# Sparse attention and feed-forward on one core: the scores of two head units joined in one TensorE segment, their loads cut by unit, and the agenda set anew

## The chip, the core and the metric

The kernel runs on one core of a Trainium2 chip. The engines of a core work side by side: TensorE (PE in the profile, its weight loads PEld) multiplies, VectorE (DVE), ScalarE (ACT) and GpSimd (POOL) do elementwise work, SyncE (SP) issues most transfers. The metric is the device time in microseconds, lower is better; the kernel before takes 816.55 us, the median of three runs.

## The reference

```python
# q, k, v: 8 batches, 8 heads, 576 positions, 64 wide; w_in 512 x 2048, w_out 2048 x 512
scores = q @ k.T / 8
local   = (0 <= i - j) & (i - j < 32)              # heads 0 to 3
strided = (0 <= i - j) & (i % 32 == j % 32)        # heads 4 to 7
attn = softmax(where(mask, scores, -1e9)) @ v
x = attn, heads side by side: 4608 tokens x 512
h = x @ w_in
g = where(h >= 1, h, where(h <= -1, 0, (h + 1)**2 / 4))
out = g @ w_out
```

All of it is float32. The kernel splits each factor of the feed-forward's products into a rounded part and a remainder and adds three products, so one product of 128 x 128 by 128 x 512 is three matmuls.

## The kernel before

**Feed-forward.** TensorE's time is mostly the feed-forward. The first three chunks of 512 tokens go the plain way (functions `up`, `gate`, `rounded`, `down`, matmuls on lines 775 and 820), one step for each of the 16 blocks of 128 hidden columns. The other 3072 tokens go in three blocks of 1024 (`up_block`, line 917; `down_block`, line 1005) by a scheme with seven products in place of eight. Its factors are read back from DRAM through a ring of seven buffers of 256 KB (tiles `wr`): each product, when done, lets SP fetch the factor that is used seven products later (`fetch_w`, line 845). The factors `kq` and `ks` are written to DRAM in the first phase (`ship`, `ship_sums`, on ACT's queue; a `ks` ship is 1 MB).

**Attention.** Batch by batch, while the feed-forward of earlier tokens runs. The heads go two and two (pairs p = 0, 1, each on two halves j = 0, 1 of the partitions), and the queries of the local and of the strided heads are cut into two units each. Counted from zero these are the units 0 and 1 (local: 12 and 6 blocks of 32 queries by 64 keys) and 2 and 3 (strided: 6 and 5 blocks of 54 keys). In the words of the change, units two and four are numbers 1 and 3. A step is a letter with a unit's number:

- `s` scores (TensorE, line 482), into two PSUM banks, one for each j
- `m` adds the mask out of PSUM into `pr` (DVE, line 542), which frees the two banks
- `x` row maximum, `a` or `b` subtracts it (POOL or DVE), `e` the exponential (ACT), `q` the sum, `p` or `k` adds the epsilon (ACT or DVE), `r` or `w` divides (POOL or DVE)
- `t` transposes blocks of 32 (DVE), `j` writes them to DRAM (SP, line 643, `there<-t`), `J` gathers them as `pT` (SP, line 654, `pT<-there`, four DMAs)
- `v` the product with the values (TensorE, line 669); `V` does units 1 and 3 in one go
- `h`, `l` copy the result out of PSUM (ACT; DVE for the remainder where one is kept)
- `Q0`, `Q2` load q and k (SP, line 418), `F0` to `F4` the values (line 431)

Batches 0 and 1 use a shorter way on TensorE for the transposes (`f`, line 609) and do v1 and v3 apart.

**Banks and buffers.** The scores and value products of all batches from 1 on share two PSUM banks, a0 and a1, taken in turn: a segment on TensorE starts only when the readers of the segment before it are done. The tile pool for q and k (`qk_p`) has two buffers. Before, each holds one pair of heads over all columns: `Q0` loads the two pairs of local heads (576 KB each) for units 0 and 1, `Q2` the two of strided heads (604 KB each) for units 2 and 3.

**Order.** All of it is written out by hand. `BEGIN` is the order of the opening; `WORK` gives each attention step of batches 1 to 7 a time, `SUMS`, `SHIP` and `CONV` those of the weights' preparation, `X_WORK` and `G_WORK` those of the splits and sums in the blocks of 1024. These times count groups of six large matmuls, from zero where the second chunk begins; 128 is the start of the blocks. `until(t)` issues every step with a time below t between two groups. The list fixes the order on every engine and in SP's queue. A step can run earlier than its time on an engine that has nothing to wait for; TensorE's steps stand where they are put, and in the blocks SP is held to TensorE's pace by the ring.

Of the kernel before, what the change touches and what calls it, by code (L numbers as in the profile page):

```python
# [28 lines left out]
BEGIN = """
Zs0:17 o0 s0 o1 i0 X0 s1 i1 S0 o3 g1 x1 s2 Zv0:3 Zf0:3 m2 e0 a1 A00 s3 i3 e1 x2 q0 p0 g3 a2 q1 Zf0:9  # L30
e2 w0 Zf0:5 f0 p1 x3 c0 B00 v0 b3 L00 e3 r1 q2 p2 f1 C00 r2 q3 A10 d1 D00 p3 h0 r3 L10 l0 A20 v1 B10
f2 h1 d2 f3 c3 v3 l1 H1 L20 C10 G10 v2 E10 M0 M1 h3 B20 l3 E00 h2 H3 C20 U0 l2 G20 V0 M3 U1 H2 M2
E20 V1
"""
# [62 lines left out]

# [1078 lines left out]
```

## Time and profile before

| what | value |
|---|---|
| median of 3 runs | 816.55 us (816.5 to 817.0) |
| profiled execution | 817.29 us |
| its span, first to last instruction | 815.5 us |
| TensorE busy | 806.2 us, 6969 matmuls |
| DVE, ACT, POOL busy | 574.7, 495.4, 232.5 us |
| moved by DMA | 195.10 MB |

The profiled execution's time is its span and 1.8 us around it. In the lines below, a group has its source line, engine, operation, output and inputs, shapes and count; in the timeline a row has its start, its length from the first start to the last end, and the instructions merged into it. Neighbouring matmuls overlap, so the next row starts before the one above it has ended, and the cost of a segment is read from start to start. A row such as `64*32 64x64` is a matmul with 64 rows and 32 columns of weights and 64 columns of data; each float32 product of the attention is two such instructions. The chain of waits lists, back from the last instruction of a window, what released each step.

### The profile page before, as it was taken

The page shows a single profiled execution, that of the slowest core. Times are in us where ns is not written, and L with a number is a line of the kernel's source. Part 1 is how long each engine was busy: PE and PEld are TensorE (multiplying, and loading weights), DVE is VectorE, ACT ScalarE, POOL GpSimd, SP SyncE. Part 2 cuts the span into 40 slices and gives each one's busy share as a digit, 9 for nine tenths or more (in the row PEclk, how much of TensorE's full clock was granted, in tenths as well). Part 3 has the DMA queues.
Part 4 walks back from the last instruction along what each step waited for, and adds up shares of the span by engine and source line. Part 5 has one row for each costly group of instructions (what it writes and reads, how often), then busy time and mean ns, then how long its engine had stood idle before and what let it go on. Part 6 is the DMA issues. An engine that isn't in the chain of part 4 may idle for free.

```text
span 815.5 us, 17861 instructions
## 1 busy us (share of the span) xinstructions
PE 806.2 (99%) x6969; PEld 656.9 (81%) x6969; DVE 574.7 (70%) x850; ACT 495.4 (61%) x866; POOL 232.5 (29%) x226
## 2 busy tenths in 40 slices
PE   8999999999999999999999999999999999999998
PEld 6788888878878888887878888888888888888886
DVE  5898868767548477776778876675589834558664
ACT  5888955545355365776775453778654647775442
POOL 5353544873347543023222000220120001114100
PEclk9999999999999999999999999999999999999999
DMA  9936437788868867987998768887666776666765
GB/s 344 408 138 201 153 111 274 265 298 278 265 221 299 286 243 257 304 287 247 285 288 266 216 203 249 263 265 228 193 193 213 232 235 196 196 192 190 216 200 170
DMA packets 101796, 195.10 MB, mean 239 GB/s; under 512 B 17105, under 2 KB 32465, under 8 KB 99665
## 3 DMA queue, kind: packets, MB, share of 16 engines
q1 hardware_dynamic: 92496, 164.60, 63.3%
q10 hardware_dynamic: 9216, 29.36, 9.4%
q8 instruction: 55, 0.90, 0.5%
q14 instruction: 29, 0.23, 0.1%
HBM read 147.26 MB, written 46.66 MB: 238 GB/s over the span
## 4 chain that ended last, share of the span: by engine, by line
PE 91%; DMA 5%; issue 1%; DVE 1%; ACT 1%; POOL 0%; SPq 0%; ACTq 0%; POOLq 0%
PE o L820 16%; PE h L775 16%; PE yo L1005 15%; PE y L917 15%; PE zo L1005 8%; PE z L917 7%; PE xo L1005 4%; PE x L917 4%; PE xp L669 3%; PE sc L482 3%; DMA wr<-kq 1%; DMA qk<-in_qk_s 1%; DMA there<-t 1%; DMA pT<-there 1%; DMA qk<-in_qk_l 1%
## 5 line engine op out<-in xcount | busy, mean ns | idle before, releaser
L917 PE MATMUL y<-x,wr 128*128 128x512 f32 x576 | 141.3, 392 | 0.0
L775 PE MATMUL h<-xq,w 128*128 128x512 f32 x576 | 140.0, 392 | 0.1
L1005 PE MATMUL yo<-hl,wr 128*128 128x512 f32 x576 | 132.8, 390 | 0.6 <-DMA wr<-kq 0.6
L820 PE MATMUL o<-gh,w 128*128 128x512 f32 x384 | 130.1, 399 | 0.0
L1005 PEld LDWEIGHTS yo<-hl,wr 128*128 128x128 f32 x576 | 108.0, 188 | 23.4 <-DMA wr<-kq 1.0
L775 PEld LDWEIGHTS h<-xq,w 128*128 128x128 f32 x576 | 107.4, 188 | 23.4 <-DVE xq L739 0.7
L917 PEld LDWEIGHTS y<-x,wr 128*128 128x128 f32 x576 | 107.4, 188 | 22.7
L820 PEld LDWEIGHTS o<-gh,w 128*128 128x128 f32 x384 | 72.1, 188 | 16.2
L820 PE MATMUL o<-gl,w 128*128 128x512 f32 x192 | 75.0, 391 | 0.0
L917 PE MATMUL z<-x,wr 128*128 128x512 f32 x288 | 73.7, 391 | 0.0
L957 POOL TENSOR_TENSOR ga<-gb,ga 128x1024 f32<-128x1024 f32 x9 | 21.6, 2397 | 167.5 <-DVE ga L785 141.7
L1005 PE MATMUL zo<-hl,wr 128*128 128x512 f32 x288 | 66.1, 390 | 0.0
L572 POOL TENSOR_TENSOR pr<-pr,st 128x384 f32<-128x384 f32 (+3 forms) x21 | 26.3, 1253 | 135.7 <-DVE st L595 64.5
L1005 PEld LDWEIGHTS zo<-hl,wr 128*128 128x128 f32 x288 | 54.0, 188 | 11.3
L917 PEld LDWEIGHTS z<-x,wr 128*128 128x128 f32 x288 | 53.8, 188 | 11.3
L782 ACT ACTIVATE tmp<-tmp 128x512 f32<-128x512 f32 x96 | 60.7, 632 | 3.0
L871 DVE TENSOR_TENSOR hl<-ga,hl 128x1024 fp32r<-128x1024 f32 x36 | 47.3, 1315 | 19.9 <-ACT hl L870 18.2
L870 ACT CAST hl<-ga 128x1024 fp32r<-128x1024 f32 x36 | 38.0, 1056 | 35.1 <-PE yo L1005 12.6
L396 POOL TENSOR_TENSOR xs<-w 128x512 f32<-128x512 f32 x32 | 45.1, 1426 | 48.4 <-DMA ks<-xs 32.8
L785 DVE SCALAR_TENSOR_TENSOR h<-h,u 128x512 f32<-128x512 f32 x47 | 32.8, 697 | 30.5 <-ACT u L782 30.1
L398 POOL TENSOR_TENSOR xs<-xs 128x256 f32<-128x256 f32 x64 | 51.3, 802 | 5.0
L779 ACT ACTIVATE u<-h,half 128x512 f32<-128x512 f32 x48 | 33.1, 689 | 29.6 <-PE h L775 24.1
(120 smaller groups left out, 1321.9 us busy)
## 6 DMA issues: line engine op xcount, KB each, us to landing
wr<-ks SPq DMA_DIRECT2D x192, 256.0 KB, 3.9
wr<-kq SPq DMA_DIRECT2D x144, 256.0 KB, 3.4
...
qk<-in_qk_s SPq DMA_DIRECT2D x16, 604.0 KB, 6.1
...
v<-in_v_l SPq DMA_DIRECT2D x21, 384.0 KB, 6.0
```

The lines of the kernel that those rows point to most:

```text
L396: nc.gpsimd.tensor_tensor(out=b[:, :, f] if i else b[:, f], in0=hi, in1=lo, op=ALU.add)
L398: nc.gpsimd.tensor_tensor(out=st[:, to, HF:], in0=st[:, x, HF:], in1=st[:, y, HF:], op=op)
L572: eng.tensor_tensor(out=pr, in0=pr, in1=st[:, 0].unsqueeze(2).broadcast_to(list(pr.shape)), op=ALU.add)
L775: nc.tensor.matmul(o_ps[c, f], wt[f][:, 0, h, x, e:e + P], xq[c][:, y, cc], start=first and n == 0, stop=last and n == len(todo) - 1)
L779: nc.scalar.activation(u, h, AF.Relu, bias=half, scale=0.5)
L782: nc.scalar.activation(u, u, AF.Square)
L785: nc.vector.scalar_tensor_tensor(out=to, in0=h, scalar=1.0, in1=u, op0=ALU.max, op1=ALU.min)
L820: nc.tensor.matmul(o_ps[c][d], wt[f][:, 1, h, x, e:e + P], gs[y], start=f == 0 and n == 0, stop=f == NF - 1 and n == 2)
L870: nc.scalar.copy(t[:, 0], src)
L871: nc.vector.tensor_tensor(out=t[:, 1], in0=src, in1=t[:, 0].bitcast(F32), op=ALU.subtract)
L917: nc.tensor.matmul(to, w_[:, a, c * P:(c + 1) * P], xc[m][:, b, c], start=m in (1, 2, 5) and c + q == 0, stop=c == 1 and q == 2, skip_grou ...
L1005: nc.tensor.matmul(to, w_[jj][:, a, d * P:(d + 1) * P], t[:, b, jj], start=m in (1, 2, 5) and k + jj + q == 0, stop=k == NP // 2 - 1 and j ...
```

## The change

From batch 2 on, the step `s3` issues the scores of unit 1 and then those of unit 3. Both lie in the same two banks: unit 1's full slot in columns 0 to 127, its half slot from column 128, unit 3's full slots from column 256, and its half slot in the same columns as unit 1's, on the other partitions. For that, unit 3's half slot swaps the halves of the partitions between j = 0 and 1 (`half_of`). The step `s1` is gone from batches 2 to 7; `m1` and `m3` stay two steps.

q and k are laid out by unit on the host: `qk_0` for unit 0 (384 columns), `qk_2` for unit 2 (334), `qk_13` for units 1 and 3 side by side (224 + 280). From batch 2 on there are three loads a batch, each for two pairs of heads: `Q0`, `Q2` and `Q3`, of 2 x 384, 2 x 342 and 2 x 516 KB. Batches 0 and 1 load as before.

The order of a batch from 2 on is then s0, s2, v0, s3 (with s1), v2, V, where it was s0, s1, s2, v0, s3, v2, V. The times in `WORK` from batch 2 on are new; so are `SUMS`, `SHIP`, `X_WORK`, `G_WORK`, a few in `CONV`, the two constants `GATE` and `ROUNDED`, and the end of `BEGIN` on DVE and ACT.

```diff
-GATE, ROUNDED = (0.31, 2.01), (1.62, 3.18)
+GATE, ROUNDED = (0.31, 1.87), (1.62, 3.26)
...
- 2: [(-13.48, 'F0'), (-11.61, 'Q0'), (-6.26, 'F1'), (0.1, 's0'), (0.19, 'm0'), ... (2.76, 's1'), ... (5.69, 'Q2'),
-     ... (10.93, 's2'), ... (17.04, 'v0'), ... (19.7, 'l0'), (20.13, 's3'), ... (37.36, 'v2'), ... (44.62, 'V1'), ...
+ 2: [(-11.46, 'Q0'), (-9.5, 'F0'), (-6.26, 'F1'), (0.1, 's0'), (0.11, 'Q2'), (0.19, 'm0'), ... (4.16, 's2'), (4.69, 'Q3'),
+     ... (16.05, 'v0'), ... (18.64, 'l0'), ... (20.17, 's3'), (21.8, 'm1'), ... (39.02, 'v2'), ... (50.62, 'V1'), ...
- 3: [(26.83, 'Q0'), (29.08, 's0'), (37.27, 'm0'), ... (40.48, 's1'), ... (43.81, 'Q2'), ... (48.59, 's2'), ...
-     (57.71, 's3 m3'), ... (59.19, 'v0'), ... (71.29, 'v2'), ...
+ 3: [(24.63, 'Q0'), (27.77, 's0'), (31.29, 'Q2'), (37.63, 'm0'), ... (40.49, 's2'), ... (43.06, 'Q3'), ...
+     (57.32, 's3'), (57.61, 'm1'), ... (57.78, 'm3'), ... (59.09, 'v0'), ... (71.0, 'v2'), ...
- 4: [(57.8, 'Q0'), (72.56, 's0'), ... (77.35, 's1'), ... (80.1, 'Q2'), ... (84.42, 's2'), ... (95.51, 's3'), ... (117.48, 'V1'), ...
+ 4: [(57.93, 'Q0'), (72.56, 's0'), ... (72.74, 'Q2'), ... (77.27, 's2'), ... (80.58, 'Q3'), ... (95.37, 's3'), ... (119.3, 'V1'), ...
- 5: [... (113.91, 's0'), ... (128.62, 'J0'), ... (135.2, 'v0'), ... (154.56, 'j3'), ... (156.06, 'J3'), ...
+ 5: [... (111.18, 's0'), ... (128.62, 'J0'), ... (134.35, 'v0'), ... (156.25, 'j3'), ... (157.1, 'J3'), ...
- 6: [... (152.17, 's0 m0 x0'), ... (158.36, 'Q2'), ... (163.66, 's2'), ... (190.07, 'j3'), ... (193.3, 'J3'), ... (198.39, 'V1'), ...
+ 6: [... (151.1, 's0'), ... (151.15, 'Q2'), ... (156.05, 's2'), (156.3, 'Q3'), ... (193.66, 'j3'), ... (194.58, 'J3'), ... (198.53, 'V1'), ...
- 7: [(183.43, 'Q0'), ... (264.44, 'J2'), ... (270.63, 'v2'), ...
+ 7: [(186.43, 'Q0'), ... (257.42, 'J2'), ... (269.93, 'v2'), ...
...
+    def half_of(u, j):
+        return 1 - j if u == 3 else j
     def seat(u, n, j):
         I = IL if UNITS[u][0] else IS
         s, i = divmod(n, I)
-        return (j, s, i) if s < UNITS[u][2] // I else (0, s, i + j * I // 2)
+        return (j, s, i) if s < UNITS[u][2] // I else (0, s, i + half_of(u, j) * I // 2)
...
+    QK = {0: qk_0, 2: qk_2, 3: qk_13}
+    COLS_1 = S - UNITS[1][1] * QL + ST
+    def load_qk(b, g, p):
+        src = QK[g][b, p]
+        t = qk_p.tile([P, 2, src.shape[2]], F32, tag="qk", name=f"qk_{b}_{g}_{p}")
+        nc.sync.dma_start(t, src)
+        for u, x in ((g, t),) if g < 3 else ((1, t[:, :, :COLS_1]), (3, t[:, :, COLS_1:])):
+            loaded[b, u, p, "qk"] = x
...
+        def score(u):
+            us = (1, 3) if b > 1 and u == 3 else (u,)
+            if len(us) > 1:
+                ts = [psum("a", [P, CH], f"sc_{b}_{u}_{j}") for j in range(2)]
+                def view(t, at, n, W):
+                    return t[:, at:at + n * 2 * W].rearrange("p (n h w) -> p n h w", h=2, w=W)
+                ahead[1, "s"] = [(view(t, 0, 1, WL), view(t, 2 * WL, 1, WL)) for t in ts]
+                ahead[3, "s"] = [(view(t, 4 * WL, 2, WS), view(t, 2 * WL, 1, WS)) for t in ts]
+            for u in us:
+                score_of(u)
...
+    U1, U3 = 12 * QL, 6 * WS
+    qk_0, qk_2 = qk_l[..., :U1], qk_s[..., :U3 + 64 - WS]
+    qk_13 = np.concatenate([qk_l[..., U1 - ST:], qk_s[..., U3:]], 4)
```

More of the change, by code (lines that the diff above doesn't have):

```diff
@@ L22 @@
 CLASSIC = 3
-GATE, ROUNDED = (0.31, 2.01), (1.62, 3.18)
+GATE, ROUNDED = (0.31, 1.87), (1.62, 3.26)
 BEGIN = """
[L30 to L33, printed above, removed]
-"""
-WORK = {1: [(-60.38, 's0'), (-55.74, 'm0'), (-55.4, 'x0'), (-52.6, 'a0'), (-51.93, 's1'), (-51.84, 'Q2'), (-51.74, 'e0 q0'),
[60 rows of a table removed]
-SUMS = [((0, 0), 30.03, 34.27, 34.91, 37.39), ((1, 1), 64.0, 67.03, 67.68, 74.53), ((0, 0), 16.76, 22.19, 23.74, 27.21),
[5 rows of a table removed]
-X_WORK = {0: [(104.12, 1), (105.35, 2), (120.26, -7), (123.3, 7), (123.54, -6), (124.89, -5), (127.46, 6), (127.6, 5),
-     (129.94, 3), (131.5, -4), (134.1, 4)],
- 1: [(196.58, 1), (203.12, 2), (203.92, -7), (211.17, 7), (211.24, -6), (216.29, -5), (218.76, -4), (220.88, 5),
-     (225.52, 6), (231.99, 3), (237.02, 4)],
- 2: [(314.25, 1), (315.57, -7), (318.67, 7), (320.48, -6), (327.96, 2), (328.63, -4), (329.29, -5), (334.12, 5),
-     (337.09, 3), (339.07, 6), (347.97, 4)]}
+Zs0:17 o0 s0 o1 i0 X0 s1 i1 S0 o3 g1 x1 s2 Zv0:3 Zf0:3 m2 e0 s3 a1 A00 i3 e1 x2 q0 p0 g3 a2 q1 Zf0:9
+e2 w0 Zf0:5 f0 p1 x3 c0 B00 v0 b3 L00 e3 r1 q2 p2 f1 C00 r2 q3 A10 d1 D00 p3 h0 r3 L10 l0 v1 B10 f2
+A20 h1 d2 f3 c3 v3 l1 H1 L20 C10 G10 v2 E10 M0 M1 h3 l3 B20 h2 E00 H3 C20 U0 l2 G20 H2 V0 M3 U1 V1
+M2 E20
+"""
+WORK = {1: [(-60.38, 's0'), (-55.74, 'm0'), (-55.4, 'x0'), (-52.6, 'a0'), (-51.93, 's1'), (-51.84, 'Q2'), (-51.74, 'e0'),
[62 rows of a table added]
+SUMS = [((0, 0), 27.43, 34.14, 34.48, 36.04), ((0, 1), 41.64, 42.75, 44.37, 45.37), ((0, 0), 20.89, 22.91, 23.78, 26.47),
[5 rows of a table added]
+X_WORK = {0: [(99.95, 2), (105.24, 1), (120.26, -7), (123.38, -6), (123.76, 7), (124.89, -5), (127.46, 6), (127.62, 5),
+     (128.98, -4), (130.46, 3), (133.39, 4)],
+ 1: [(188.28, 1), (202.28, -7), (203.39, 2), (210.65, 7), (211.24, -6), (212.76, -5), (217.38, -4), (220.5, 5),
+     (224.44, 6), (225.88, 3), (237.31, 4)],
+ 2: [(314.63, 1), (318.5, -7), (320.68, 7), (320.87, -6), (327.96, 2), (328.59, -5), (328.74, -4), (334.45, 5),
+     (337.29, 3), (338.84, 6), (349.14, 4)]}
 CONV = [(-63.99, 'L0.1'), (-63.97, 'A0.1 B0.1'), (-63.52, 'A1.1'), (-63.03, 'C0.1'), (-62.58, 'A3.0'), (-62.43, 'D0.1'),
@@ L132 @@
  (-23.81, 'B12.0'), (-23.64, 'L11.1'), (-23.56, 'B11.1'), (-23.42, 'L13.0'), (-23.33, 'C12.0'), (-23.26, 'C11.1'),
[2 rows of a table removed]
[2 rows of a table added]
  (-18.75, 'D13.0'), (-18.25, 'C12.1'), (-17.87, 'A14.0'), (-17.83, 'D12.1'), (-16.23, 'E13.0'), (-16.16, 'L14.0'),
[4 rows of a table removed]
[4 rows of a table added]
  (-8.08, 'C15.1'), (-7.92, 'D15.1'), (-7.81, 'E15.1')]
-G_WORK = {0: [(165.99, 's11'), (167.56, 's10'), (183.93, 's12'), (187.61, 's20'), (187.74, 's13'), (188.3, 't60'),
[26 rows of a table removed]
-SHIP = [[1.27, 12.82, 7.42, 20.53, 13.61, 18.54, 30.97, 29.74, 34.32, 31.23, 40.56, 58.58, 43.6, 47.29, 57.58, 63.72],
- [67.18, 66.59, 57.74, 75.26, 81.54, 83.67, 98.23, 100.97, 96.76, 104.83, 107.05, 116.41, 110.54, 116.4, 120.59,
+G_WORK = {0: [(166.13, 's11'), (171.17, 's10'), (184.17, 's12'), (185.93, 's13'), (186.58, 's20'), (186.8, 't60'),
[26 rows of a table added]
+SHIP = [[1.76, 9.43, 4.16, 9.04, 7.71, 16.78, 30.13, 28.39, 27.95, 31.89, 43.05, 58.54, 41.31, 47.29, 57.58, 59.69],
+ [65.08, 59.34, 57.19, 75.01, 81.48, 84.8, 98.23, 98.51, 98.16, 100.44, 109.9, 118.16, 110.44, 117.42, 120.59,
   125.26]]
@@ L178, in tile_sparse_attention_then_ffn @@
     qk_s: bass.AP,
+    qk_0: bass.AP,
+    qk_2: bass.AP,
+    qk_13: bass.AP,
     v_l: bass.AP,
@@ L189, in tile_sparse_attention_then_ffn @@
     nc = tc.nc
-    B, _, _, _, S = qk_l.shape
+    B = qk_0.shape[0]
     DM, NT = out.shape
+    S = NT // B
     NF = w.shape[0]
@@ L410, in tile_sparse_attention_then_ffn, with load_pair @@
     loaded = {}
-    def load_qk(b, p):
+    QK = {0: qk_0, 2: qk_2, 3: qk_13}
+    COLS_1 = S - UNITS[1][1] * QL + ST
+    def load_pair(b, p):
         src = qk_l[b, p] if p < 2 else qk_s[b, p - 2]
@@ L418, in load_qk @@
         nc.sync.dma_start(t, src)
-        loaded[b, p, "qk"] = t
+        first = (0, S - COLS_1) if p < 2 else (0, UNITS[3][1] * WS)
+        for u, c in zip((0, 1) if p < 2 else (2, 3), first):
+            loaded[b, u, p % 2, "qk"] = t[:, :, c:]
+    def load_qk(b, g, p):
[4 more added lines that the diff above has]
+            loaded[b, u, p, "qk"] = x
     def load_v(b, u, k=None):
@@ L433, in load_v, with fetch_qk @@
             loaded[b, local, b0 + n] = t[:, n]
-    def fetch_qk(b, p0):
-        for p in (p0, p0 + 1):
-            if b < B and (b, p, "qk") not in loaded:
-                load_qk(b, p)
+    def fetch_qk(b, g):
+        for p in range(2):
+            if b < B and (b, g, p, "qk") not in loaded:
+                (load_pair(b, g + p) if b < 2 else load_qk(b, g, p))
     def fetch_v(b, *parts):
@@ L446, in attention @@
     def attention(b, kinds):
-        probs, flipped, there, ahead, covered = {}, {}, {}, {}, set()
+        probs, flipped, there, ahead, whole, covered = {}, {}, {}, {}, {}, set()
         def banks(u, kind):
@@ L467, in zero @@
                 nc.tensor.matmul(t[:, :N], zeros, zeros[:, :1].broadcast_to([P, N]), start=True, stop=True)
-        def score(u, pairs=range(2)):
-            local, b0, nb = UNITS[u]
-            Q, W, I, p0 = (QL, WL, IL, 0) if local else (QS, WS, IS, 2)
-            if 0 in pairs:
-                probs[u] = banks(u, "s"), W
-            sc = probs[u][0]
-            for p in pairs:
-                for n in range(nb):
-                    q0 = (b0 + n) * (QL if local else WS)
-                    k0 = max(q0 - ST, 0) if local else q0
-                    for j in range(2):
-                        _, s, i = seat(u, n, j)
-                        qk = loaded[b, p0 + p, "qk"][j * D:(j + 1) * D]
-                        nc.tensor.matmul(sc[j][i * Q:(i + 1) * Q, s, p], qk[:, 0, q0:q0 + Q],
-                                         qk[:, 1, k0:k0 + W], start=u not in covered,
-                                         stop=u not in covered)
@@ L486, in score_0 @@
-        def score_0(u):
-            score(u, (0,))
-        def score_1(u):
-            score(u, (1,))
+        def score(u):
[8 more added lines that the diff above has]
+                score_of(u)
@@ new lines, in score_of @@
+        def score_of(u):
+            local, b0, nb = UNITS[u]
+            Q, W, I = (QL, WL, IL) if local else (QS, WS, IS)
+            sc = banks(u, "s")
+            if not isinstance(sc[0], tuple):
+                n = slots(u)[1]
+                whole[u] = sc
+                sc = [(t[:, :n], t[:, n:] if n < t.shape[1] else None) for t in sc]
+            probs[u] = sc, W
+            first_col = (max(b0 * QL - ST, 0) if local else b0 * WS)
+            todo = [(p, n, j) for p in range(2) for n in range(nb) for j in range(2)]
+            for p, n, j in todo:
+                q0 = (b0 + n) * (QL if local else WS)
+                k0 = max(q0 - ST, 0) if local else q0
+                q0, k0 = q0 - first_col, k0 - first_col
+                _, s, i = seat(u, n, j)
+                last = s >= slots(u)[1]
+                qk = loaded[b, u, p, "qk"][j * D:(j + 1) * D]
+                nc.tensor.matmul(sc[j][last][i * Q:(i + 1) * Q, s - last * slots(u)[1], p], qk[:, 0, q0:q0 + Q],
+                                 qk[:, 1, k0:k0 + W], start=u not in covered,
+                                 stop=u not in covered)
@@ L501, in cover @@
             local, b0, _ = UNITS[u]
-            sc, W = probs[u]
+            W = probs[u][1]
             n = slots(u)[0]
             m = m_loc[:, b0 and 1:][:, :n].unsqueeze(2) if local else m_str.unsqueeze(1).unsqueeze(1)
-            for t in sc:
+            for t in whole[u]:
                 nc.tensor.matmul(t, ident_b, m.broadcast_to([P, n, 2, W]), start=False, stop=True)
@@ L524, in homes @@
             if ns[0] > ns[1]:
-                todo += [(j, slice(j * 64, j * 64 + 64), ns[1], ns[0], ns[1]) for j in range(2)]
+                todo += [(j, slice(h * 64, h * 64 + 64), ns[1], ns[0], ns[1]) for j, h in ((j, half_of(u, j)) for j in range(2))]
             pieces_ = []
@@ L528, in homes @@
                 of = part, slice(2 * at, 2 * (at + s1 - s0))
-                pieces_.append((sc[j][part, s0:s1], pr[of].rearrange("p (n h) w -> p n h w", h=2), part, of[1]))
+                pieces_.append((sc[j][s0 >= ns[1]][part, s0 - ns[1] * (s0 >= ns[1]):s1 - ns[1] * (s0 >= ns[1])], pr[of].rearrange("p (n h) w -> p n h w", h=2), part, of[1]))
             return room, st, pr, pieces_
@@ L745, in in_two @@
             return lambda u: do(u, rest if b == 0 else None)
-        steps = {"s": score, "y": score_0, "z": score_1, "m": mask, "o": opened, "i": cover, "g": plain, "X": most_there, "S": below_there, "x": most, "w": norm_v, "a": below_max, "e": expo, "q": total, "p": plus_eps, "k": plus_eps_v, "b": below_max_v, "r": norm,
+        steps = {"s": score, "m": mask, "o": opened, "i": cover, "g": plain, "X": most_there, "S": below_there, "x": most, "w": norm_v, "a": below_max, "e": expo, "q": total, "p": plus_eps, "k": plus_eps_v, "b": below_max_v, "r": norm,
                  "f": flip, "t": turn, "j": spread, "J": gather, "c": keep, "d": keep_v, "v": value, "V": values_1_3, "h": in_two(high, False), "l": in_two(low, False), "H": in_two(high, True), "M": in_two(low, True),
@@ L1043, in tile_sparse_attention_then_ffn @@
     with tc.manual_schedule():
-        for p in range(4):
-            load_qk(0, p)
-        load_w(0, 0, loaded[0, 1, "qk"][0:1, 0, 0:1])
+        for g in (0, 2):
+            fetch_qk(0, g)
+        load_w(0, 0, loaded[0, 0, 1, "qk"][0:1, 0, 0:1])
         load_v(0, 0)
@@ L1053, in tile_sparse_attention_then_ffn @@
         stage(4)
-        for p in range(2):
-            load_qk(1, p)
+        fetch_qk(1, 0)
         stage(6)
@@ L1154, in _layout @@
     w = np.concatenate([w_in, w_out.reshape(DFF // P, P, DM)], 2)
-    return {"qk_l": qk_l, "qk_s": qk_s, "v_l": v_l, "v_s": v_s, "w": w}
+    return {"qk_l": qk_l[:2], "qk_s": qk_s[:2], "qk_0": qk_0, "qk_2": qk_2, "qk_13": qk_13, "v_l": v_l, "v_s": v_s, "w": w}
 def kernel(**inputs):
```

198 rows, old and new, of tables (CONV, G_WORK, SUMS, WORK) are left out of this document.

## The prediction

> **What bounds the kernel.** I read the page first, then the waits of TensorE, then its timeline around the attention's short matmuls, then the chain of waits in the few places where such a segment is longer than its like.
>
> ```profile
> span 815.5 us, 17861 instructions
> PE 806.2 (99%) x6969; PEld 656.9 (81%) x6969; DVE 574.7 (70%) x850; ACT 495.4 (61%) x866; POOL 232.5 (29%) x226
> ```
>
> TensorE is busy 806.2 of 815.5 us: the idle 9.3 us, the opening and the end included, are all that a wait shown as idle could give back. DVE, ACT and POOL have room. So the time changes by what TensorE's own stream costs, and by waits that hide inside "busy", where a segment of short matmuls is stretched. No matmul is removed: the 116 score products a batch stay. What can shrink is the cost of going from 512-column matmuls to short ones and back, and waits inside segments. Next, TensorE's timeline in batch 7, where units two (x48 of 64*32) and four (x40 of 64*64) are scored apart:
>
> ```profile
> 503.05 1.52 PE L917 MATMUL z<-x,wr 128*128 128x512 f32 x6
> 504.50 0.77 PE L482 MATMUL sc<-qk 64*32 64x64 f32 x48
> 505.20 3.03 PE L917 MATMUL y<-x,wr 128*128 128x512 f32 x12
> 508.06 1.52 PE L917 MATMUL x<-x,wr 128*128 128x512 f32 x6
> 509.43 1.52 PE L917 MATMUL z<-x,wr 128*128 128x512 f32 x6
> ...
> 530.03 0.92 PE L482 MATMUL sc<-qk 64*64 64x54 f32 x40
> 530.88 1.66 PE L917 MATMUL x<-x,wr 128*128 128x512 f32 x6
> 532.37 1.52 PE L917 MATMUL z<-x,wr 128*128 128x512 f32 x6
> ```
>
> Undisturbed, six large matmuls take 1.36 us from start to start (508.06 to 509.43); that is one unit of the agenda, and below a "unit" is always this. Six before a segment take 1.45 (503.05 to 504.50), so entering costs 0.09. Twelve after one take 2.86 instead of 2.72 (505.20 to 508.06), six take 1.49 (530.88 to 532.37), so leaving costs 0.13. That is 0.22 us a segment beside the short matmuls.
>
> **The merged segment.** From batch 2 on, unit four's scores follow unit two's in one segment: six segments fewer in all. The trace has the same join for the values, where step V takes units two and four together, while batch 1 takes them apart:
>
> ```profile
> 83.97 0.90 PE L669 MATMUL xp<-pT,v 64*64 64x32 f32 x48
> 84.80 0.50 PE L820 MATMUL o<-gh,w 128*128 128x512 f32 x1
> ...
> 106.44 0.81 PE L669 MATMUL xp<-pT,v 54*64 54x64 f32 x40
> 107.19 2.11 PE L775 MATMUL h<-xq,w 128*128 128x512 f32 x8
> ...
> 562.56 1.51 PE L669 MATMUL xp<-pT,v 64*64 64x32 f32 x88
> 564.00 1.66 PE L917 MATMUL z<-x,wr 128*128 128x512 f32 x6
> ```
>
> Apart, the short matmuls hold TensorE 0.83 and 0.75 us (to the next large one's start), together 1.44: 0.14 less, and with the 0.22 of one entry and exit 0.36 a batch. This is the nearest row, but there all weights are 64 columns wide; the merged scores go from 64*32 to 64*64, which no row shows. If that step costs a whole drain, only the 0.22 is left. Between 0.22 and 0.36 I take 0.30, nearer to the join that the trace shows: 6 x 0.30 = 1.8 us less (1.3 to 2.2).
>
> The Trainium skill, TensorEngine Tiling (Array Packing), Key Properties, states that a change of the tiling mode drains TensorE. By that rule the step inside the merged segment drains once more, and this term would be 1.3 us; the join of the values, which has no such change, doesn't contradict it.
>
> The flip of the half slot in unit four moves which rows write which half of the bank; the tiles are used as often as before, so I put it at nothing. Masks for both units now follow one segment:
>
> ```profile
> 187.12 0.99 DVE L542 TENSOR_TENSOR pr<-sc,m_loc 128x128 f32<-128x128 f32 x4
> 211.16 1.15 DVE L542 TENSOR_TENSOR pr<-sc,m_str 128x216 f32<-128x216 f32 x4 [2.21 <-PE sc L482]
> ```
>
> 0.99 + 1.15 = 2.14 us of DVE before both banks are free. The tightest user is batch 3's v0, two units (2.72) after s3: hidden, 0.6 left. What is queued behind them on DVE, the gate of the step, feeds matmuls eight units later. The swaps between engines (a/b, p/k, r/w) are hidden likewise.
>
> **Waits that the new agenda takes away.** Four segments of before are longer than their like:
>
> ```profile
> 176.20 1.52 PE L775 MATMUL h<-xq,w 128*128 128x512 f32 x6
> 177.81 1.38 PE L669 MATMUL xp<-pT,v 54*64 54x64 f32 x48
> ...
> 546.06 1.39 PE L669 MATMUL xp<-pT,v 54*64 54x64 f32 x48
> 96.60 0.93 PE L669 MATMUL xp<-pT,v 54*64 54x64 f32 x48
> 386.10 1.25 PE L482 MATMUL sc<-qk 64*64 64x54 f32 x48
> 513.60 0.92 PE L482 MATMUL sc<-qk 64*64 64x54 f32 x48
> 153.30 1.08 PE L482 MATMUL sc<-qk 64*64 64x54 f32 x40
> 177.24 0.94 DVE pr L542 x2
> 379.97 6.77 DMA qk<-in_qk_s
> ```
>
> Batch 2's v2 (177.81) is 0.45 longer and starts 0.16 late (1.61 after 176.20): the chain puts batch 3's m0 on DVE before it, which held the banks. v2 goes from 37.36 to 39.02 with m0 at 37.63, so m0 is over: 0.61 back. Batch 7's v2 (546.06) is 0.46 longer; the chain has the gather J2 before it, which goes from 264.44 to 257.42 while v2 stays within a unit: back. Batch 6's s2 (386.10) waited 0.33 for q and k, issued behind gathers; Q2 now stands right behind s0 at 151.15, five units ahead of s2: back. Batch 2's s3 (153.30) is 0.16 longer, by the order of DVE behind l0, which frees its banks; l0 now moves ahead of a chunk step's rounding (19.7 to 18.64): back. Sum 1.56; the bound from below is 0.
>
> The one wait for ring weights lies behind batch 7's first q and k:
>
> ```profile
> 428.49 2.34 PE L1005 MATMUL yo<-hl,wr 128*128 128x512 f32 x9 [0.62 <-DMA wr<-kq]
> 420.84 7.61 DMA wr<-kq
> v<-in_v_s SPq DMA_DIRECT2D x8, 320.0 KB, 4.3
> v<-in_v_l SPq DMA_DIRECT2D x21, 384.0 KB, 6.0
> ```
>
> That load shrinks from 2 x 576 to 2 x 384 KB: of 0 to 0.62 I take half, 0.3.
>
> **Waits that it may add.** The loads go from four DMAs and 2.36 MB a batch to six and 2.44 (384, 342 and 516 KB each, twice): two more issues on SP. Only two q/k buffers exist, so unit three's load waits for s0, and s2 comes soon: in batches 2 and 4 four units behind s0, 5.44 us plus the entry. The second issue starts 0.45 after the first. Of like size are the rows of 320 KB (4.3) and 384 KB (6.0); so it needs 4.8 to 6.5, and s2 waits 0 to 0.9 in each. The old pairs of 604 KB in the same places (first the window 123 to 128, then 235 to 244):
>
> ```profile
> qk<-in_qk_s SPq DMA_DIRECT2D x2, 604.0 KB, 4.2
> qk<-in_qk_s SPq DMA_DIRECT2D x2, 604.0 KB, 5.7
> ```
>
> The larger load took 4.2 in batch 2: no wait there. In batch 4 a 1 MB ship runs beside it and is now at 72.11, right ahead of Q2 at 72.74: I take 0.3. The Trainium skill, DMA: Bandwidth & Descriptors, "Issuing engines are not separate DMA queues", states that DMAs issued by ACT and SP interleave on the same 16 engines; by it the ship delays Q2 though another queue issues it, and the trace agrees (5.7 against 4.2).
>
> Batch 5's v0 comes one unit earlier (135.2 to 134.35), its gather J0 stays at 128.62:
>
> ```profile
> 332.54 1.85 SPq L654 DMA_DIRECT2D pT<-there x4
> DMA to landing us min/median/max: 4.8/5.0/5.1
> 339.64 1.60 PE L669 MATMUL xp<-pT,v 64*64 64x32 f32 x96
> ```
>
> The fourth gather starts at about 334.0 and lands at 339.0; v0, one unit of 1.36 before 339.64, would start at 338.3: 0.7 if nothing moves, 0 if SP gets there sooner; I take 0.5. Batch 6's V is alike: the spread of unit four goes from 190.07 to 193.66, two units later in SP's order, V stays:
>
> ```profile
> 431.28 0.90 SPq L643 DMA_DIRECT2D there<-t x2
> 434.58 1.74 SPq L654 DMA_DIRECT2D pT<-there x4
> DMA to landing us min/median/max: 3.2/3.5/3.6
> 441.64 1.51 PE L669 MATMUL xp<-pT,v 64*64 64x32 f32 x88
> ```
>
> Landed at 435.9 + 3.6 = 439.5, plus 2.72 is 442.2, 0.6 behind V's start, but unit two's 0.83 of matmuls come first: of 0 to 0.6 I take 0.2. The ring: Q3 (2 x 516 KB) stands in batch 6 between the spread (156.25) and the gather (157.1) of batch 5, the ring's fetches behind both. Seven buffers cover 7 x 1.36 = 9.5 us; a fetch that takes 7.6, as above, leaves 1.9. I take 0.2, the bound is 3.0.
>
> **Sum**, against the profiled execution: 817.29 us, of which 815.5 are the span. -1.8 - 1.56 - 0.3 + (0.3 + 0.5 + 0.2 + 0.2) = -2.5. That execution lies 0.74 above the median of 816.55, so I forecast 814.0. The opening's steps keep their order on TensorE: nothing. What the records show longer without a cause (s0 and v0 of batch 6, 0.3 to 0.4 each) I leave in.
>
> **Rivals.** (1) The join drains and the new waits equal the old: -1.3 - 1.56 - 0.3 + 2.4 gives -0.8, 815.8. For it: all added waits stand at places with under 1 us of slack. Against it: the removed ones have named causes that are gone. 27%. (2) Slower: SP's order starves the ring. In batches 5 to 7 the gather of units two and four now waits directly behind its spread, with Q3 or Q0 ahead; a stall of about 1.9 us (one fetch behind 1 MB) in three places, beyond the sum, is +5.7: 819.7. It decides from 4.1 us of added stalls on (2.5 + 1.6). For it: the one ring wait of before came this way. Against it: it is 0.62 us only, and the largest loads of before (2 x 604 KB) were larger than Q3. 11%. (3) All waits vanish and none is added: -2.2 - 1.56 - 0.62, 812.2, and 811.4 with the two unexplained ones. Against it: J0 of batch 5. 12%. My forecast holds the remaining 50%.
>
> **Chances.** A difference under 0.2% (1.6 us) can't be told from no change here: faster means under 814.9, slower over 818.2. My forecast's own range, with its terms moved inside their bounds, is 812.5 to 814.9, so it and (3) are the chance of faster, 0.62; (1) is the chance of the same, 0.27, with a range of 814.9 to 818.2; (2) that of slower, 0.11. The range 811.4 to 817.6 reaches from the lower end of (3) through most of (1); some 5% lie below it and 13% above.
>
> **What would show it.** In the profile after: six sc segments fewer, merged ones of about 1.6 us with x88; entry 0.09 and exit 0.13 unchanged; batch 2's and 7's v2 back at 0.93; batch 5's v0 and batch 4's s2 longer than 1.60 and 0.92. Wrong, if x88 takes over 1.8, or if TensorE's waits name wr more than once.

## The result and the profile after

The changed kernel took **827.25 us** (median of 5 runs, 822.2 to 830.1) against 816.99 for the kernel before on the same chip: ratio **1.0112** (95% interval 1.0069 to 1.0155), slower by 1.1%. The forecast was 814.0, with a chance of 0.62 for faster and 0.11 for slower; it was wrong. The profiled execution took 827.82, its span is 826.0, 10.5 us above the 815.5 of before. TensorE's idle time grew from 9.3 to 15.8 us, and the page and the list of TensorE's waits say on what:

```profile
span 826.0 us, 17894 instructions
...
PE 810.2 (98%) x6969; PEld 661.3 (80%) x6969; DVE 577.6 (70%) x856; ACT 497.5 (60%) x864; POOL 226.0 (27%) x222
```
```profile
PE xp L706 <- DMA pT<-there: 6.1, 8, 1.6
PE xp L706 <- issue: 1.3, 2, 1.0
```

The products with v (L706; L669 before) waited 8 times for a gather, 6.1 us in all; in the kernel before no row of that list was over 1.0. No wait for wr is left. The rows are of this one execution; another profile of the same kernel (the run again, below) has its waits partly in other places. TensorE's timeline shows where, first step V of batch 4, then V of batch 6 (in brackets the idle time before a row and what ended it):

```profile
310.59 0.90 PE L706 MATMUL xp<-pT,v 64*64 64x32 f32 x48
312.80 0.33 PE L706 MATMUL xp<-pT,v 54*64 54x64 f32 x4 [1.31 <-DMA pT<-there]
314.62 1.30 PE L706 MATMUL xp<-pT,v 54*64 54x64 f32 x36 [1.50 <-DMA pT<-there]
315.85 4.04 PE L812 MATMUL h<-xq,w 128*128 128x512 f32 x12
...
447.55 0.90 PE L706 MATMUL xp<-pT,v 64*64 64x32 f32 x48
450.02 0.33 PE L706 MATMUL xp<-pT,v 54*64 54x64 f32 x4 [1.56 <-DMA pT<-there]
450.85 1.04 PE L706 MATMUL xp<-pT,v 54*64 54x64 f32 x36 [0.50 <-DMA pT<-there]
451.82 4.53 PE L1042 MATMUL yo<-hl,wr 128*128 128x512 f32 x13
```

Unit two's 48 products run at once; unit four's 40 wait for its gather J3. From the first short matmul to the next large one it is 5.26 and 4.27 us instead of 1.44. And the large ones behind are slow: 12 take 4.04 where the prediction's row behind a segment has 3.03. The table by stretches gives the granted clock (PEclk, the third column from the end):

```profile
core 0: us, PE busy (x) PEld busy (x) DVE busy (x) ACT busy (x) POOL busy (x), PEclk, DMA share, GB/s
310.00:315.70 5.70, 2.90 (x91) 2.31 (x90) 1.40 (x3) 1.04 (x2) 3.68 (x6) 0.91 0.76 244
315.70:317.70 2.00, 2.00 (x11) 1.52 (x6) 0.39 (x1) 1.63 (x11) 0.00 (x0) 0.50 0.42 82
452.00:455.00 3.00, 3.00 (x8) 2.37 (x9) 0.00 (x0) 1.34 (x10) 0.00 (x0) 0.56 0.91 331
455.00:458.00 3.00, 3.00 (x14) 2.46 (x14) 0.71 (x1) 1.80 (x2) 0.00 (x0) 1.00 0.36 109
```

Behind each long wait the clock is at 0.50 and 0.56 for 2 to 3 us: 1.0 us lost behind batch 4's V, 1.3 behind batch 6's. Smaller waits of the same kind stand at v0 of batches 5 and 6 (344.56 and 404.24; batch 7's has one of 0.17), and batch 2's merged segment waits for the read of its banks:

```profile
154.51 0.30 PE L525 MATMUL sc<-qk 64*32 64x64 f32 x2 [0.26 <-DVE xq L776]
...
344.56 1.59 PE L706 MATMUL xp<-pT,v 64*64 64x32 f32 x92 [0.24 <-DMA pT<-there]
...
404.24 0.30 PE L706 MATMUL xp<-pT,v 64*64 64x32 f32 x4 [0.49 <-DMA pT<-there]
404.87 1.59 PE L706 MATMUL xp<-pT,v 64*64 64x32 f32 x92 [0.33 <-DMA pT<-there]
```

Counted from large matmul to large matmul against the kernel before, the account of the span is: V of batch 4 +3.8 and +1.0 at half clock; V of batch 6 +2.8 and +1.3; v0 of batches 3, 5, 6, 7 +0.6, +0.5, +0.9, +0.7 (the wait in batch 3's has no releaser in the profile); s3 of batch 2 +0.6 (it is 0.8 over a whole one, and was 0.2 over its like before); V of batch 2 +0.1; the opening +1.8. Together +14.1. Gone: the merge's 6 x 0.23 = 1.4, v2 of batches 2 and 7 (0.6, 0.5), s0 and s2 of batch 6 (0.4, 0.3), the wr wait (0.9), together -4.1; s0 is 0.02 longer in each batch (+0.1). The sum is +10.1 of the 10.5; where the other 0.4 lies the rows don't show.

**Why the gathers were late.** SP's timeline, batch 4, the kernel before and then the changed one:

```profile
295.09 0.90 SPq L643 DMA_DIRECT2D there<-t  x2
...
297.19 2.22 SPq L654 DMA_DIRECT2D pT<-there  x4
```
```profile
296.62 0.90 SPq L680 DMA_DIRECT2D there<-t  x2
299.11 0.94 SPq L441 DMA_DIRECT2D qk<-in_qk  x2
300.14 2.92 SPq L691 DMA_DIRECT2D pT<-there  x4
303.16 0.89 SPq L680 DMA_DIRECT2D there<-t  x2
307.70 3.97 SPq L691 DMA_DIRECT2D pT<-there  x4
```

Before, unit two's spread and gather stood at 93.09 and 96.69 in batch 4, some 18 units ahead of unit four's, and only unit four's pair stood ahead of V. Now that both units are scored together, j1, J1, j3, J3 (111.48 to 117.02) stand in one row on SP, batch 5's Q2 among them, and each gather waits for the landing of its spread. The time that the agenda leaves between J3 and V shrank as well, from 113.84 and 117.48 to 117.02 and 119.3: from 3.6 units to 2.3, or 3.1 us. The chain of waits ends with these links:

```profile
303.16 4.52 DMA there<-t
...
309.02 5.47 DMA pT<-there
```

The landings of unit four's gathers (80 KB) also got slower. From the list of DMA issues, before and after (KB each, median us from issue to landing):

```profile
pT<-there SPq DMA_DIRECT2D x24, 80.0 KB, 3.2
```
```profile
pT<-there SPq DMA_DIRECT2D x24, 80.0 KB, 5.0
```

This is the last link before V. Unit two's gathers (48 KB) did not get slower: 3.7 before, 3.1 after.

### The profile page after: what moved, and what is told of

Its sections match the earlier page's. It is cut to its first block, busy times and chain, and to the rows that moved or that the text cites. A ratio compares the mean times of both kernels' runs of the same rounds, so it can differ in the third digit from the quotient of the medians.

```text
span 826.0 us, 17894 instructions
## 1 busy us (share of the span) xinstructions
PE 810.2 (98%) x6969; PEld 661.3 (80%) x6969; DVE 577.6 (70%) x856; ACT 497.5 (60%) x864; POOL 226.0 (27%) x222
## 4 chain that ended last, share of the span: by engine, by line
PE 85%; DMA 8%; SPq 2%; DVE 1%; issue 1%; ACT 1%; POOL 1%; DVEq 0%; POOLq 0%
PE yo L1042 15%; PE o L857 14%; PE h L812 14%; PE y L954 14%; PE zo L1042 8%; PE z L954 7%; PE x L954 3%; PE sc L525 3%; DMA pT<-there 3%; PE xp L706 3%; PE xo L1042 3%; DMA there<-t 2%; SPq L691 1%; DMA ks<-xs 1%; DMA qk<-in_qk_l 1%
## 5 line engine op out<-in xcount | busy, mean ns | idle before, releaser
L812 PE MATMUL h<-xq,w 128*128 128x512 f32 x576 | 142.3, 396 | 0.0
L812 PEld LDWEIGHTS h<-xq,w 128*128 128x128 f32 x576 | 109.1, 191 | 23.8 <-DVE w L378 0.4
L609 POOL TENSOR_TENSOR pr<-pr,st 128x540 f32<-128x540 f32 (+3 forms) x19 | 23.5, 1236 | 140.8 <-DVE st L605 140.3
L908 DVE TENSOR_TENSOR hl<-ga,hl 128x1024 fp32r<-128x1024 f32 x36 | 43.9, 1222 | 22.0 <-ACT hl L907 21.7
L408 POOL TENSOR_TENSOR xs<-xs 128x256 f32<-128x256 f32 x64 | 54.1, 845 | 5.0
```

The lines of the kernel that those rows point to most:

```text
L408: nc.gpsimd.tensor_tensor(out=st[:, to, HF:], in0=st[:, x, HF:], in1=st[:, y, HF:], op=op)
L812: nc.tensor.matmul(o_ps[c, f], wt[f][:, 0, h, x, e:e + P], xq[c][:, y, cc], start=first and n == 0, stop=last and n == len(todo) - 1)
L908: nc.vector.tensor_tensor(out=t[:, 1], in0=src, in1=t[:, 0].bitcast(F32), op=ALU.subtract)
```

## The experiments

My theory: the loss is lateness on SP's queue (spreads, gathers, v and ring loads bunched before V and v0), with the half clock on top. The rivals: the merged segment or its masks cost; the loads by unit cost; the opening costs. Times are medians, and the ratio is to the kernel before on the same chip. The runs are from several chips, on which the kernel before had medians of 816.7 to 818.1, so runs of different sections are best compared by their ratios.

**pairs.** Agenda of the changed kernel:

```diff
-4: (107.69,'w3') (111.48,'j1') (113.39,'J1') (113.52,'t3') (114.1,'j3') (117.02,'J3')
+4: (107.69,'w3') (107.7,'t3') (111.48,'j1') (111.49,'j3') (113.39,'J1') (113.5,'J3')
-6: (189.46,'w3') (190.51,'J1') (191.2,'t3') (193.66,'j3') (194.58,'J3')   7: (186.43,'Q0')
+6: (189.46,'w3') (189.47,'t3') (190.0,'J1') (191.5,'j3') (194.2,'J3')    7: (195.0,'Q0')
```

> The changed kernel with another order of the late steps of batches 4 and 6 alone: in batch 4 the transposes and spread of unit four (t3, j3) stand directly behind those of unit two (t1, j1) and ahead of the gather J1; in batch 6 t3, j3 and J3 move forward by about two units and batch 7's first load of q and k (Q0) moves behind them. V stays where it is. Main theory (the gathers of V land late because spread, gather, spread, gather stand one behind another in SP's queue, and each wait of about 3 us also halves TensorE's clock for some 2 us): both V segments fall from 5.58 and 4.58 us to about 1.8, and the half-rate matmuls behind them go, so 3.8 + 2.8 + 2 x 1.1 = 8.8 us less, about 818.4 against the changed kernel's 827.2. Rival (the merged segment and its masks, or the loads by unit, cost the time, and the waits at V are only where it shows): the wait moves to the next segments and the time stays within 2 us of 827.

Measured 821.19 (8 runs), ratio 1.0048 (1.0028 to 1.0069): 5 to 6 us back of the 8.8 expected, with two transposes, two spreads, three gathers and one load at other times and nothing else changed. V of batches 4 and 6 in its timeline:

```profile
312.36 1.51 PE L706 MATMUL xp<-pT,v 64*64 64x32 f32 x88
313.80 2.56 PE L812 MATMUL h<-xq,w 128*128 128x512 f32 x10
...
446.67 0.33 PE L706 MATMUL xp<-pT,v 54*64 54x64 f32 x4 [0.88 <-DMA pT<-there]
447.59 0.80 PE L706 MATMUL xp<-pT,v 54*64 54x64 f32 x36 [0.59 <-DMA pT<-there]
448.32 1.88 PE L1042 MATMUL yo<-hl,wr 128*128 128x512 f32 x7
```

Batch 4's V is whole again (1.44). Batch 6's still waits 1.5 us, so that half of the expectation failed: the gather there took 6 us. (In the agenda its J3 moved by 0.4 units, not by two.) The rival of "the waits only move" is out as the whole of it. What the edit gave at each V is not shown by this one profile; see the run again.

**q2late.** `-5: (113.21,'Q2')` becomes `(117.1,'Q2')`, behind batch 4's J3.

> The changed kernel with one step moved: batch 5's second load of q and k (Q2), which waits on SP for the scores of batch 5's unit one, goes from ahead of batch 4's J1 to behind its J3. Rival theory (the loads by unit do the harm, since Q2 holds SP's queue until s0 has run and takes the DMA engines): batch 4's V segment falls from 5.58 to about 1.8 us and the slow matmuls behind it go, 4.9 us less. Main theory (the chain is spread, gather, spread, gather, each waiting for the landing of the one before; J1 could start only 0.3 to 0.8 us sooner without Q2): the segment falls by 0.5 to 1.5 us and stays over 4, and the time by 1 to 2 us.

Measured 824.31 (10 runs), ratio 1.0084 (1.0055 to 1.0113): 2 to 3 us less, between the two, but its interval overlaps that of the changed kernel. In its timelines V is whole, and v0 of the next batch waits instead:

```profile
296.32 0.90 SPq L680 DMA_DIRECT2D there<-t  x2
298.35 2.92 SPq L691 DMA_DIRECT2D pT<-there  x4
301.32 0.94 SPq L680 DMA_DIRECT2D there<-t  x2
303.48 2.99 SPq L691 DMA_DIRECT2D pT<-there  x4
```
```profile
310.58 1.51 PE L706 MATMUL xp<-pT,v 64*64 64x32 f32 x88
...
339.65 0.30 PE L706 MATMUL xp<-pT,v 64*64 64x32 f32 x4 [0.42 <-DMA pT<-there]
340.44 1.59 PE L706 MATMUL xp<-pT,v 64*64 64x32 f32 x92 [0.48 <-DMA pT<-there]
```

From the issue of j1 to that of J3 it is 7.2 us here (296.32 to 303.48), against 11.1 in the first profile of the changed kernel (296.62 to 307.70). But most of that difference is not Q2's: in the run again, whose steps stand as in the changed kernel, it is 8.5 (298.23 to 306.70 below). Against that, Q2 ahead of J1 costs 1.3 us at J3, within the 0.5 to 1.5 expected of V, though J1 itself starts 1.7 us sooner without it, not 0.3 to 0.8. So Q2 is a link of the chain, and the loads by unit have that share in the lateness; most of the rest of the 11.1 is the spread that landed 4.5 us after its issue.

**again.** The changed kernel unaltered, for a second profile.

> The changed kernel itself once more, for a second profile of it. Main theory: the gathers in front of V of batches 4 and 6 and of v0 of batches 5 to 7 are so close to their use that single executions differ by what the DMA engines happen to do, so V of batch 4 (5.6 us in the first profile, 1.8 in that of the run 'opening', which has the same steps there) can be anywhere from 1.8 to 5.6, and the time from 818 to 830. Rival: the same places with the same lengths each time, within 0.5 us.

Measured 823.75 and 831.87. In this profile V of batch 4 is whole, and V of batch 6 waits less (SP's rows of batch 4 first, then TensorE's):

```profile
298.23 0.90 SPq L680 DMA_DIRECT2D there<-t  x2
...
306.70 3.26 SPq L691 DMA_DIRECT2D pT<-there  x4
```
```profile
312.46 1.51 PE L706 MATMUL xp<-pT,v 64*64 64x32 f32 x88
...
447.81 0.33 PE L706 MATMUL xp<-pT,v 54*64 54x64 f32 x4 [0.95 <-DMA pT<-there]
```

Instead v2 of batch 2 and s2 of batch 3 are 1.9 and 1.7 us longer. So a single clean V proves little (those of pairs and q2late included): the steps stand so close to their data that each execution is late somewhere else. Counted from large matmul to large matmul, V of batch 4 took 5.26, 1.44 and 1.44 us, and V of batch 6 4.27, 3.41 and 2.38, in the profiles of the changed kernel, of again and of opening, which have the same agenda from batch 2 on. The account above is one draw of several; what all three share is a wait for a gather at V of batch 6. In the seven runs of the changed kernel the time went from 822 to 832.

**fill.** Zero matmuls between unit two's and unit four's products of V, 20 in batch 4 and 13 in batch 6:

```diff
 for u, (n, q) in zip(us, size):
+    if u == 3 and b in (4, 6):
+        for _ in range(20 if b == 4 else 13):
+            nc.tensor.matmul(xp[0][:, at:at + n * q], zeros, ..., start=True, stop=True)
     value(u, ...)
```

> The changed kernel with zero matmuls (20 in batch 4, 13 in batch 6, into the part of the bank that is overwritten right after) put between unit two's and unit four's products of step V, where TensorE waits for the gather. They add work, but only inside the wait (about 2.1 of 2.8 us, and 1.4 of 2.0). If the half clock behind V comes from TensorE standing idle, the slow matmuls behind both V segments go and the time falls by about 2 x 1.1 = 2.2 us, with the V segments themselves as long as before (5.6 and 4.6). Rival (the half clock has another cause, or the wait's end is set by what follows): the segments grow or the slow matmuls stay, and the time is the same or up to 1 us longer.

Measured 825.01 (4 runs), ratio 1.0106 (1.0070 to 1.0141): by the ratio nothing clear against the changed kernel's 1.0112. Batch 4 in the timeline, and the clock behind:

```profile
310.65 2.93 PE L718 MATMUL xp<-zeros 128*128 128x320 bf16 x20
313.51 0.81 PE L706 MATMUL xp<-pT,v 54*64 54x64 f32 x40
314.25 3.04 PE L815 MATMUL h<-xq,w 128*128 128x512 f32 x12
```
```profile
314.90:316.90 2.00, 2.00 (x10) 1.61 (x9) 0.99 (x1) 1.09 (x9) 0.00 (x0) 1.00 0.58 134
```

The half clock is gone with TensorE kept busy, as expected of idleness. But unit four's products ran without a gap behind the fillers, and V of batch 4 took 4.43 us, not 5.3: the gather may have landed sooner by itself, and the fillers then cost what they saved. The test is in line with the theory and does not prove it.

**opening.** The opening's list of steps and the convolution's times put back to those of before.

> The changed kernel with the opening's order and the convolution steps' times of the kernel before (the two lists from the start up to the first down products), the rest as changed. The profiles showed the first large matmul 0.9 us later in the changed kernel and then 12 instead of 5 or 6 matmuls at half rate, about 0.8 us. If the new order of the opening is the cause, the first large matmul comes at 24.1 again and the time falls by 0.9 to 1.7 us. If it was chance of one execution, the same within 0.5 us at that place.

Measured 827.85 (10 runs, 818.1 to 836.2, the profiled one 818.14), ratio 1.0100 (1.0068 to 1.0132): nothing gained. The same pair on a calmer kernel, early and early_open below, gives 822.02 and 822.15. The first large matmul starts at 24.06 us in the kernel before and at 24.96 in the first profile of the changed kernel, but at 23.75 in the run again, with the new order, and at 24.82 in opening, with the old. So the 1.8 us of the first profile do not come from the new order.

**early, early_open.** `early` is pairs with more time for the late steps: J0 of batches 5 to 7 sooner, v0 of batches 3, 5, 7 and s3 of batch 2 later, batch 6's j1, t3, j3, J3 two units sooner, and the opening of before.

> The changed kernel, its computation and its merged segment as they are, with the late steps given time in every batch where TensorE waited: batch 4's and 6's spreads ahead of the gathers as in the run with pairs, in batch 6 also two units sooner; J0 of batches 5, 6 and 7 issued 0.7 to 1.3 units sooner; v0 of batches 3, 5 and 7 0.6 to 0.85 units later; batch 2's s3 0.8 units later, behind the read that frees its banks; and the opening of the kernel before. Main theory (late gathers, nothing else): V of batch 6 falls from 3.5 to 1.8, v0 of batches 5, 6, 7 from 2.2, 2.8, 2.3 to 1.85 or less, s3 of batch 2 from 2.4 to 1.85: about 5 us under the run with pairs (821.2), so 816, and below the kernel before in the same comparison by 1 to 3 us (the merged segments' 6 x 0.21 plus the stalls of before that are gone, 1.5). Rival (the merge or the loads by unit cost by themselves): it stays 2 us or more above the kernel before.

> The kernel 'early' with the changed kernel's opening instead of that of the kernel before. The profiles so far have the opening (first large matmul, and what the matmuls behind it lose at half rate) at 24.4 us in the kernel before, 25.0 to 26.2 in four of the changed kernel's kind, 25.2 with the opening of before. If the new order there costs, it is 0.5 to 1.5 us slower than 'early'; if that is chance, the same within 0.5.

Measured 822.02 (10 runs), ratio 1.0053 (1.0023 to 1.0084), and 822.15, ratio 1.0060 (1.0031 to 1.0089). By its number early missed: it stays more than 2 us above the kernel before, where the rival had put it. All V and the v0 of batches 3, 5 and 7 are whole, but two of my moves made new waits: J0 of batch 5 held SP ahead of the ring's first fetches (three waits for wr behind 328 us, 0.4 to 0.5 of idle time each), and batch 6's v0 now waited for a v load that I had put behind J0.

**early2, early3, early4.** Each mends what the profile of the one before showed. early2: J0 of batch 5 behind those fetches, batch 5's V 1.6 units sooner, since it frees the v buffers. early3: batch 6's 1 MB Q3 from 157.2 to 167.0 and batch 7's Q0, F0, F1 7 to 17 units later. early4: v0 and s3 of batch 6, s2 of batch 3, s3 of batch 1 later by 0.6 to 2 units.

> The kernel 'early' with its own three new waits mended: batch 5's J0 goes back behind the seven ring fetches that open the first Winograd block (at 127.9 it held SP until its spread had landed, and TensorE waited 2.2 to 3.2 us for wr); batch 6's second v load (F1) stands ahead of J0 again, with batch 5's V 1.6 units sooner (it frees the v buffers) and batch 6's v0 0.85 later; batch 6's Q3, which holds SP until s2 has run, goes behind batch 5's J3; s0 of batch 3 1.2 units and s3 of batch 2 0.9 units later. Main theory (nothing but lateness in SP's queue and what follows it): v0 of batch 6 falls from 3.2 to 1.85 and the wr waits of about 2.7 us go, 4 to 5 us under 'early' (822.0): 817 to 818, level with the kernel before or up to 2 us below it. Rival (the merge or the loads by unit cost by themselves, or move the waits on without end): 820 or more.

Measured 822.60, ratio 1.0060 (1.0037 to 1.0083): missed, with the number in the rival's range again. Its profile shows gathers that take 6.4 to 7.9 us ahead of batch 6's v0, in a stretch with a DMA share of 1.06 and 373 GB/s (the last two columns):

```profile
390.00:398.00 8.00, 7.76 (x33) 5.68 (x31) 4.97 (x9) 6.95 (x20) 1.60 (x1) 1.00 1.06 373
```

> The kernel 'early2' with the DMA traffic of batch 6 thinned where its profile shows landings of 7 to 8 us (388 to 400 us, DMA share 1.06): batch 6's Q3 (1 MB) goes from 157.2 to 167.0, behind J0 and the v loads; batch 7's Q0, F0 and F1 go 6 to 17 units later (they are wanted from 228.8 on); batch 2's h0 and l0 ahead of a sum step that held ACT and DVE (s3 of batch 2 was 1.3 us late for them); s3 of batch 7 0.4 units later. Main theory (late transfers in a crowded stretch): the ring waits behind 386 us (1.4), v0 and s3 of batch 6 (1.6 + 1.0), s3 of batch 2 (1.3) and the wait behind V of batch 6 (1.2) go for the most part, 4 to 6 us under 'early2' (822.6): 817 to 818.5. Rival (each mended place only passes the lateness on, as the total has not fallen from 'pairs' over 'early' to 'early2'): 820 to 823 again.

Measured 819.31, ratio 1.0024 (1.0008 to 1.0041): about 3 us less with the traffic thinned and batch 2's h0 and l0 moved, just above the range expected.

> The kernel 'early3' with three more segments given time: v0, s3 and J2 of batch 6 one to two units later (v0 still waited 1.35 us for gathers that took 6 us beside the v loads, and s3 1.2 us for the copies that free its banks), s2 of batch 3 0.8 later (it waited 0.8 us for the read of its banks), s3 of batch 1 0.6 later (0.9 us in most runs). Main theory: these 3.3 to 4.2 us go, 815 to 816 against 819.3, and 1 to 2.5 us below the kernel before in the same comparison. Rival (the lateness is only passed on): 818 to 820, above the kernel before.

Measured 818.71, ratio 1.0023 (1.0004 to 1.0042): by the ratio nothing gained, as the rival had it. The mended segments are whole but for batch 6's v0 (still 0.55 longer), and one new wait stands behind batch 6's merged segment. Its two masks held DVE 2.2 us in a row, the sums of the blocks of 1024 queued behind them, ACT's copy of such a sum came late, and TensorE waited for it:

```profile
415.63 1.65 PE L954 MATMUL z<-x,wr 128*128 128x512 f32 x6 [1.30 <-ACT gab L989]
```

**early5, early5_apart, and the merge by itself.** early5 parts these two masks in the agenda and changes almost nothing else. The kernels named apart take the merge out of the same kernel:

```diff
-us = (1, 3) if b > 1 and u == 3 else (u,)
+us = (u,)        # and 's1', 'm1', 'x1' 1.5 to 4 units behind 's3' in the agenda
```

> The kernel 'early4' with one mend: in batch 6 the mask of unit four goes 2.4 units behind that of unit two (in 'early4' both stood in a row, 2.2 us of DVE from 405.9 to 408.1, and the large matmuls behind waited 1.65 us for sums queued behind them), and v0 0.1 later. If the masks in a row were the cause, that wait goes: 1 to 1.7 us under 'early4' (818.7), 817 to 817.7, level with the kernel before. If not, 818.5 to 819.5 again.

> The kernel 'early5' with units two and four scored apart. If the merge gains what its segments show, 1.3 us slower than 'early5' (0.5 to 2); if masks in a row and the hop eat the gain, the same within 0.5 or faster.

early5 measured 817.77 (12 runs, 817.2 to 819.5), ratio **0.9995** (0.9978 to 1.0011): the loss of the changed kernel is gone, with its computation, its merged segment and its loads kept and only the agenda altered. Its longest wait at that place:

```profile
PE z L954 <- ACT gab L989: 0.5, 1, 0.5
```

early5_apart measured 820.12, ratio 1.0038 (1.0024 to 1.0052): without the merge 2.3 us slower. The two earlier pairs agree in sign:

> The kernel 'early' with units two and four scored apart again (unit four alone at the place of the merged segment, unit two in a segment of its own 1.5 to 4 units later, with its mask and maximum moved behind it); the loads by unit stay. If the merge is worth what the segments of the changed kernel show (1.86 against 0.79 + 0.94 + 0.22 re-entries, and 0.025 less on s0 which has no hop), this one is 6 x 0.21 = 1.3 us slower than 'early'. If the merge costs something (masks of two units in a row, the hop), it is as fast or faster.

> The kernel 'early2' with units two and four scored apart again, as in 'early_apart'. If the merge is worth the 0.21 us a batch of the segments, 1.3 us slower than 'early2' (within their scatter, 0.5 to 2.5); if the merge costs, as fast or faster.

Measured 824.24 against 822.02, and 824.05 against 822.60: 2.2 and 1.5 us. So the rival that the merge costs is out, except for its masks where they stand in a busy stretch of DVE. But 1.5 to 2.3 us is not the size of its gain: all three kernels named apart have, in batch 5, a wait that their altered agenda made, for unit four's mask ahead of unit two's segment. From early5_apart:

```profile
347.02 1.04 PE L525 MATMUL sc<-qk 64*32 64x64 f32 x48 [1.10 <-DVE pr L579]
```

The segments by themselves give 6 x 0.23 = 1.4 us (below); the expectations took 0.21 a batch. No run has the merged segment with the loads of before, so what the loads by unit cost by themselves, beyond Q2's place, was not measured.

**early6.** Three more waits given time (s3 of batch 6, s2 of batch 3, s3 of batch 1).

> The kernel 'early5' with three segments 0.7 to 1 unit later, behind the copies that free their banks: s3 of batch 6 and its first mask, s2 of batch 3 with its mask, s3 of batch 1 with its mask. If lateness is all that is left, 1.5 to 3 us go: 815 to 816.3 where 'early5' had 817.8, and below the kernel before by 0.1 to 0.4%. If the lateness is passed on once more, the same within 0.7 of 'early5'.

Measured 817.52 (12 runs, 815.4 to 821.1), ratio 1.0001 (0.9982 to 1.0020): nothing more, so the lateness was passed on. No version beat the kernel before beyond its interval.

## Why the prediction was wrong, step by step

- **The step that failed** is "Waits that it may add". I named batch 5's v0 (0.5 taken, 0.5 measured), batch 4's s2 (0.3 taken, 0 measured) and for batch 6's V "of 0 to 0.6 I take 0.2"; that V cost 2.8 and 1.3 at half clock. Batch 4's V I did not list at all; it cost 3.8 and 1.0. In place of the 1.2 us that the sum has for all added waits, the profile shows 8.9 at these two V alone. I took the issue of the gather and its landing (3.2 to 3.6) from the profile of before, where unit two's pair had long been done. I moved unit four's spread by two units in SP's order but did not follow unit two's, which the merge makes just as late, so that its spread and gather stand ahead of unit four's. In batch 4 unit four's two links then took 4.5 and 5.5 us, with 3.1 us left by the agenda between J3 and V. That such a link is late belongs to the agenda; how late it is differs from execution to execution (V of batch 4 was whole in two other profiles). The half clock behind a wait was no term of the prediction at all.
- **The boundary**, 6 x 0.30, was 6 x 0.23, next to its lower bound of 0.22. The merged segment in TensorE's timeline:

```profile
539.88 1.61 PE L525 MATMUL sc<-qk 64*32 64x64 f32 x88
541.42 1.66 PE L954 MATMUL x<-x,wr 128*128 128x512 f32 x6
```

  It holds TensorE 1.54 us; apart it was 0.70 and 0.85 in the prediction's rows. The join saves next to nothing inside (0.01), unlike that of the values (0.14); only one entry and exit are saved. The Trainium skill, TensorEngine Tiling (Array Packing), Key Properties, states that a change of the tiling mode drains TensorE. By that rule this term was 1.3 us, and the trace agrees: 1.4.
- **The waits taken away** went as forecast in the profiled execution: batch 2's and 7's v2 0.6 and 0.5, batch 6's s2 0.3, the ring's wait 0.9 (0.3 taken), and s0 of batch 6 came back 0.4 besides. Batch 2's v2 did not stay whole: in the profiles of again and pairs it waited 1.34 and 1.55. Batch 2's s3 was to improve by 0.16 and got 0.8 longer: l0 does stand sooner, but on DVE it stayed behind a sum step that waited for ACT, and ACT for POOL.
- **The ring**, rival (2), did not starve in the changed kernel. That rival had the right engine, SP's order, and the right sign, with the wrong victim: the gathers of V and v0, not the fetches of wr. Neither of the two signs of being wrong came (x88 at 1.6 us, no wait for wr): both looked at the terms that held.
- **The loads.** The list of DMA issues after has them at 384, 334 and 504 KB each; the 342 and 516 of the text ahead are too large, while the 2.44 MB fits the smaller ones. In the kernel before, the 1 MB ship (issued at 236.80, 6.7 us to landing) had all but landed when batch 4's load was issued at 243.20; what ran beside that load were two kq writes of 256 KB from ACT's queue (242.04). In the changed kernel ship and Q2 do overlap (235.19 and 238.72), Q2 landed after 4.9 to 5.3 us, and s2 had no wait: the 0.3 taken for it was put on a reading that the trace doesn't bear out.
- **The masks** were hidden in the changed kernel as said; "What is queued behind them on DVE" cost 1.3 us once the segment stood elsewhere (early4).

What stays open: early5 and early6 are level with the kernel before, though the merge should gain 1.4 us in them and the waits of before that the new agenda was to take away come to about 2 more. Their profiles show scattered waits of 0.5 to 1 us for copies and loads that differ from run to run; which of them belong to the change, and whether the loads by unit have a part in them, was not settled.
